# Cross-partition sums and maxima moved from GpSimd to TensorE, and snapshots issued ahead of weight steps

## The chip, the cores and the metric

The kernel runs on one core of a Trainium2 chip. The metric is the device time of one execution in microseconds. The median of three runs of the kernel before is 1585.49 us (1582.71 to 1587.73).

## The reference, cut to what matters

Attention (2 x 8 heads, 768 positions, 64 dimensions, masked to equal clusters) gives x of 1536 x 512. Two networks follow:

```
h = x @ w_in;  x = (h * clip(h + 3, 0, 6) / 6) @ w_out          # first network, w_in 512 x 2048
P = exp(x @ w_gate - max)                                       # 1536 x 8
for _ in range(8):                                              # balancing
    P /= P.sum(1) + 1e-9;  P /= P.sum(0) + 1e-9;  P *= N / E
out = sum over 8 experts e of P[:, e] * (relu(x @ w1[e]) @ w2[e])   # w1: 512 x 1024, w2: 1024 x 512
```

Matrices are multiplied as f16 pairs: a high half and the rest (lo), scaled by a power of two that is taken from the largest absolute value of the whole tensor. So each tensor needs a maximum over all 128 partitions, and each round of balancing a sum over all partitions for 8 columns.

## The kernel before, in words

All engines run their own queues in the order in which the program issues (a manual schedule); an instruction that waits holds all behind it on its engine.

**First network.** w_in and w_out are handled in two halves (n = 0, 1) of 1024 hidden columns. Half 0 runs 24 steps of its first layer (`l1_mm`, then `act2` of the step before and `act1`; L1277 to 1285) and then 24 steps of its second layer (`layer2`, L1307 to 1315). Half 1 does both in one loop with a lag of two steps (L1463 to 1484). Beside them a list `todo` prepares the next weights: load, decode, maximum (`amax`), scale, high and low halves. `run_todo` (L1001) issues in each step a share of the list by listed costs. `hops` (L1013) issues the first part of a maximum in one step, pauses a step or two, and issues all other parts together in one later step (`run`).

A maximum over partitions has two forms. `top_library` (L115): one `partition_all_reduce` on GpSimd (L122), then the scale on VectorE. `top_steps` (L93): VectorE writes each partition's maximum to a column of `pad`; TensorE transposes `pad` into PSUM (`red_rows`, L76); VectorE takes the maximum of each row (`red_max`, L81); TensorE broadcasts the one wanted to all partitions (`to_all`, L86); VectorE computes the scale. Attention uses `top_steps` for the first w_in; all later maxima use `top_library`.

**Experts.** A step n (L1693 to 1721) issues: evacuations of the last step (`evac`), 12 matmuls of the first layer (`l1_part`, L1606 to 1609), 12 of the second layer of a unit 14 steps back (`l2_part`, L1558 to 1560, from step 14 on), the parts of the activation that fall due (`early`), the list `run_todo` (n < 14) and the planned functions `plan2` of the step (weights of coming experts, x2, balancing), and last `post`: snapshots of PSUM sums to SBUF on ScalarE (L1667) and sums on VectorE (L1670 to 1679). An expert takes 42 steps. `l1_part` two steps on writes into a sum again that `post` has copied. Weights: `pre` scales on ScalarE (L1352, L1417), differences and low halves run on GpSimd (L1364 to 1383, L1430, L1438), high halves on ScalarE (L1379, L1434).

**x2 and balancing.** Three blocks of x are scaled anew for the second network (`x2_tasks`): two inside half 1, the third in steps 5 to 25 of the expert loop. `balance_tasks` runs at steps 27 to 51: a maximum over the logits, then eight rounds of `row` (VectorE), `total` (`partition_all_reduce`, L1179, on GpSimd) and `col` (VectorE, which begins with the sum).

Of the kernel before, what the change touches and what calls it, by code (L numbers as in the profile page):

```python
# [31 lines left out]
def attention_moe_kernel(  # L32
# [53 lines left out]
        nc.tensor.matmul(  # L86
            ps, lhsT=r.to_broadcast([P, P]), rhs=ident[:, col:col + ps.shape[1]], start=start, stop=True, skip_group_check=True)

    def sum_all(x, ps):

        nc.tensor.matmul(ps, lhsT=one.to_broadcast([P, P]), rhs=x, start=False, stop=True, skip_group_check=True)

    def top_steps(cols, col, name, room, then):  # L93

# [76 lines left out]
    def spare(n):  # L171
        return spare_columns(n)
# [46 lines left out]
    def weight_tasks(n, m, pool, raw=None):  # L219

        src = layers[n][m]
        wide = src.dtype != F32
        rows, cols = src.shape
        nr = rows // P
        NP = 8
        d = {}
        nm = f"w{n}_{m}"

        def view(t, i):

            return t.rearrange("p a f -> p (a f)")[:, 512 * i:512 * (i + 1)]

        def start():
            d["raw"] = raw
            if raw is None:
                d["raw"] = mp.tile([P, nr, cols], F32, tag="raw", name=f"{nm}_raw", bufs=1)
            d["mx"] = small.tile([P, NP], F32, tag="w_mx", name=f"{nm}_mx")
            if not wide:
                nc.sync.dma_start(d["raw"], src.rearrange("(c p) f -> p c f", p=P))

        def load(i):
            r, o = divmod(512 * i, cols)
            d["c", i] = wide_tile(
                wdec2, src[P * r:P * r + P, o:o + 512].bitcast(U32), f"{nm}_c{i}", [512], bufs=WB)

        def dec0(i):
            d["t", i] = decode0(wdec2, d["c", i], f"{nm}_t{i}", bufs=3)

        def dec1(i):
            decode1(d["t", i])  # L250

        def dec2(i):
            decode2(d.pop(("c", i)), d["t", i], view(d["raw"], i))


        sums = wide and m == 1

        def amax(i):
            if sums:
                nc.scalar.activation(  # L260
                    d.pop(("t", i)).bitcast(F32), view(d["raw"], i), AF.Abs, accum_out=d["mx"][:, i:i + 1])
                return
            nc.vector.tensor_reduce(
                d["mx"][:, i:i + 1], view(d["raw"], i), axis=AX.X, op=ALU.max, apply_absolute_value=True)

        def scale1(m1):
            d["s"], wsc[n, m] = scale_of(m1, 1, 12 if sums else 2 + m, f"ws{m}", small, bufs=4)
            if pool is wpool:
                wsp[n, m] = pool.tile([P, 2, nr, cols], F16, tag="ws", name=f"{nm}_s", bufs=1)
            else:  # L270
                wsp[n, m] = wring[:, 4 * n:4 * n + 4].rearrange("p b x -> p (b x)").rearrange(
                    "p (z r c) -> p z r c", z=2, r=nr)

        def hi(i):
            nc.scalar.activation(view(wsp[n, m][:, 0], i), view(d["raw"], i), AF.Copy, scale=d["s"][:, 0:1])

        def lo(i):
            nc.vector.scalar_tensor_tensor(
                out=view(wsp[n, m][:, 1], i), in0=view(d["raw"], i), scalar=d["s"][:, 0:1],
                in1=view(wsp[n, m][:, 0], i), op0=ALU.mult, op1=ALU.subtract)  # L280

        def piece(i):
            if not wide:
                return idle, idle, idle, idle, lambda: amax(i), idle
            return (lambda: load(i), lambda: dec0(i), lambda: dec1(i), lambda: dec2(i), lambda: amax(i), idle)

        def lo_pool(i):

            v = view(d["raw"], i)
            nc.scalar.activation(v, v, AF.Copy, scale=d["s"][:, 0:1])  # L290
            nc.gpsimd.tensor_tensor(out=view(wsp[n, m][:, 1], i), in0=v, in1=view(wsp[n, m][:, 0], i), op=ALU.subtract)

        parts = []
        for i in range(NP):
            parts += [(0.05, lambda i=i: hi(i)), (0.2, lambda i=i: lo_pool(i)) if (n, m) == (1, 0) else (0.7, lambda i=i: lo(i))]
        scale = top_library(lambda: d["mx"], nm, scale1)
        return start, [("m", piece(i)) for i in range(NP)], scale, parts

    def pipeline(pieces, depth):
# [713 lines left out]
    def hops(steps, turns=1):  # L1013

        def pause():
            pass

        def run():
            for f in steps[1:]:
                f()  # L1020

        far.append(pause)
        return [(0.2, steps[0])] + [(0.0, pause)] * turns + [(1.3, run)]
# [8 lines left out]
    def gate_weights():  # L1032
# [14 lines left out]
            nc.vector.scalar_tensor_tensor(  # L1047
                out=wg[:, 1], in0=raw, scalar=wgs["s"], in1=wg[:, 0], op0=ALU.mult, op1=ALU.subtract)

        return [(0.05, g0), (0.3, g1)] + hops(top_library(lambda: mx, "wg", g1s)) + [(0.3, g2)]  # L1050

    cfac = {}

# [25 lines left out]
    def x2_tasks(bk, room):  # L1079
# [57 lines left out]

        q11, q12, q21, q22 = (0, 0), (0, 1), (1, 0), (1, 1)
        first = [(0.65, lambda h=h, g=g: amax(h, g)) for h in range(2) for g in range(2)]
        top = top_library(lambda: d["mx"], f"x2_{bk}", sc1)  # L1140
        hl = lambda o, v: ([(0.1, hi(o, v))], [(0.7, lo(o, v))])
        order = [
            hl(B11, q11), hl(B21, q21), hl(B22, q22), hl(T1, q11), hl(T3, q12), hl(T2, q22), hl(T4, q21)]
# [12 lines left out]
    def balance_tasks():  # L1156
# [18 lines left out]
            d["cs"] = cs  # L1175

        def total():
            d["ct"] = small.tile([P, NE], F32, tag="b_sum", name="b_sum")
            nc.gpsimd.partition_all_reduce(d["ct"], d.pop("cs"), channels=P, reduce_op=RED.add)  # L1179

        def col(more):
            ct = small.tile([P, NE], F32, tag="b_ct", name="b_ct")
            nc.vector.tensor_scalar(out=ct, in0=d.pop("ct"), scalar1=1e-9, scalar2=None, op0=ALU.add)
            nc.vector.reciprocal(ct, ct)
            nc.vector.tensor_scalar(out=ct, in0=ct, scalar1=float(NT * P) / NE, scalar2=None, op0=ALU.mult)
            nc.vector.tensor_tensor(pr, pr, ct.unsqueeze(1).to_broadcast([P, NT, NE]), op=ALU.mult)
            (row if more else fin)()

# [142 lines left out]
    def expert_w1(e):  # L1331
# [22 lines left out]
        def pair(i):  # L1354
# [33 lines left out]

        return (
            load, [(0.65, lambda i=i: amax(i)) for i in range(8)],  # L1390
            top_library(lambda: d["mx"], f"w{n}_0", scale1), [(0.3, lambda i=i: pre(i)) for i in range(8)],
            [pair(i) for i in range(4)])

    def expert_w2(e):
# [41 lines left out]
        def lo(k, h):  # L1436
# [3 lines left out]

        return (
            load, [(0.3, lambda i=i: amax(i)) for i in range(8)],
            top_library(lambda: d["mx"], f"w{n}_1", scale1), [(0.3, lambda i=i: pre(i)) for i in range(8)],
            diff, hi, lo)

    def parts2(diff, hi, lo):
# [91 lines left out]

    hq, po2, evacs2 = {}, {}, []

    def spare_columns(n):
        return bank(5, "lg2", (n,)), True

    def l2_part(n):

# [135 lines left out]

    first, top, rest = x2_tasks(NBK - 1, spare)
    for n, (_, f) in enumerate(first):
        at2(5 + n, f)
    at2(9, top[0])
    at2(10, top[1])
    for n, (_, f) in enumerate(rest):
        at2(11 + n // 2 if n < len(rest) - 1 else 25, f)
    for n, f in enumerate(balance_tasks()):
        at2(27 + 4 * n // 3, f)  # L1690
    todo += ops2[20:]
    NU2 = 2 * NPASS
    for n in range(PASS * (NPASS + 1)):  # L1693
# [19 lines left out]
                early(u - 1, k + 7)  # L1713
        if u < NU2 and k in (2, 5, 6):
            early(u, k)
        if n < PASS and todo:
            run_todo(max(1, PASS - 3 - n))
        for f in plan2.pop(n, []):
            f()
        if u < NU2:  # L1720
            post(u, k)
    while evacs2:
        evac(*evacs2.pop(0))
    assert not plan2
# [31 lines left out]
```

## Time and profile before

| | |
|---|---|
| median of three runs | 1585.49 us |
| the profiled execution's own time | 1587.1 us |
| its span | 1585.3 us |
| TensorE matmuls, busy share of the span | 88% |
| VectorE, ScalarE, GpSimd | 66%, 57%, 45% |
| mean granted TensorE clock | 0.951 |

The engines are PE (TensorE), DVE (VectorE), ACT (ScalarE), POOL (GpSimd). In the page's 40 slices of 39.6 us TensorE is busy nine tenths or more from slice 21 to slice 39; ahead of that slices 15, 18, 19 and 20 show 5 to 6 tenths, and in the same four the granted clock falls to 7 tenths (counted from 1, read from the left).

### The profile page before, as it was taken

The numbers are of one execution on the slowest core, as the hardware profiler recorded it, in microseconds if no ns is written. First come the engines' busy times: TensorE is split into PE (matmuls) and PEld (weight loads), VectorE is DVE, ScalarE is ACT, GpSimd is POOL, SyncE is SP. The second block draws the span as 40 slices with busy tenths as digits, with TensorE's granted clock in tenths as the row PEclk, the third lists the DMA queues.
The fourth block names the chain that finished last, engine by engine and source line by source line (L and its number), as shares of the span: only waits on it lengthen the run. The fifth ranks groups of instructions, "written<-read, shape, count | busy, mean of one in ns | idle before, by whom it ended". The sixth has DMA issues, their size and how long they took to land.

```text
span 1585.3 us, 30485 instructions
## 1 busy us (share of the span) xinstructions
PE 1390.5 (88%) x12342; PEld 1070.8 (68%) x12342; DVE 1048.0 (66%) x1968; ACT 911.1 (57%) x1633; POOL 714.7 (45%) x721
## 2 busy tenths in 40 slices
PE   3788787898989857965699999999999999999997
PEld 1456565443434326853587888888888888888886
DVE  7788888767755525752467667667676676676664
ACT  3677777464644455442466755756756746756641
POOL 1679889542201555033163363355346426416600
PEclk9999889998999978977799999999999999999999
DMA  9576543322310011000110110110110111011001
GB/s 223 128 157 128 107 87 65 102 94 68 106 53 1 1 53 54 2 1 1 53 39 16 54 47 8 54 54 2 54 54 5 51 54 54 2 55 54 8 28 47
DMA packets 112236, 88.08 MB, mean 56 GB/s; under 512 B 79328, under 2 KB 95712, under 8 KB 112096
## 3 DMA queue, kind: packets, MB, share of 16 engines
q1 hardware_dynamic: 112096, 86.15, 20.1%
q8 instruction: 96, 1.57, 0.4%
q14 instruction: 44, 0.36, 0.1%
HBM read 64.01 MB, written 3.15 MB: 42 GB/s over the span
## 4 chain that ended last, share of the span: by engine, by line
PE 49%; DVE 21%; ACT 12%; issue 9%; POOL 6%; DMA 1%; SPq 0%; DVEq 0%; POOLq 0%; ACTq 0%
PE oX L1558 4%; PE oX L1560 4%; PE oX L1559 4%; PE X L1606 4%; PE X L1608 4%; PE X L1609 4%; DVE pmt L681 3%; PE oY L1558 3%; PE oY L1560 3%; PE oY L1559 3%; ACT w_raw L1352 2%; PE l L1248 2%; ACT w_raw L1417 2%; PE Z L1606 2%; PE Z L1609 2%
## 5 line engine op out<-in xcount | busy, mean ns | idle before, releaser
L748 POOL TENSOR_TENSOR El<-E,Eh 128x384 f16<-128x384 f32 x192 | 189.5, 1017 | 74.4 <-DVE Eh L744 40.6
L1438 POOL TENSOR_TENSOR wring<-w_raw,wring 128x512 f16<-128x512 f32 x112 | 129.3, 1159 | 141.8 <-ACT wring L1434 134.3
L1606 PE MATMUL X<-xop,wop 128*128 128x256 f16 x576 | 160.3, 278 | 30.8 <-ACT snap L1667 24.7
L1608 PEld LDWEIGHTS <-wop 128*128 128x128 f16 x1344 | 133.3, 99 | 71.8 <-issue 54.7
L1577 DVE SCALAR_TENSOR_TENSOR acc<-oX,coef,acc 128x256 f32<-128x256 f32 x168 | 81.0, 482 | 128.5 <-PE oX L1560 118.4
L1608 PE MATMUL X<-xop,wop 128*128 128x256 f16 x576 | 160.4, 278 | 0.0
L1609 PE MATMUL X<-xop,wop 128*128 128x256 f16 x576 | 160.1, 278 | 0.0
L1609 PEld LDWEIGHTS <-wop 128*128 128x128 f16 x1344 | 133.4, 99 | 17.9 <-POOL wop L1383 0.5
L1606 PEld LDWEIGHTS <-wop 128*128 128x128 f16 x1344 | 133.5, 99 | 17.6
L122 POOL PARTITION_ALL_REDUCE w_m<-w_mx x19 | 7.5, 393 | 271.4 <-DVE w_mx L1343 156.4
L735 ACT ACTIVATE E<-pS,esc 128x768 f32<-128x768 f32 x96 | 86.2, 899 | 68.1 <-PE pS L731 46.7
L1606 PE MATMUL Z<-xT,wop 128*128 128x256 f16 x384 | 105.9, 276 | 20.0 <-ACT snap L1667 18.0
L1558 PE MATMUL oX<-wring,a 128*128 128x256 f16 x384 | 105.9, 276 | 16.8 <-ACT acc L1571 12.7
L1615 ACT ACTIVATE a<-a 128x512 f16<-128x512 f32 x96 | 57.4, 598 | 109.7 <-DVE a L1645 71.2
L1615 ACT ACTIVATE q<-u 128x512 f16<-128x512 f32 x96 | 57.1, 595 | 101.9 <-DVE u L1673 77.4
L1558 PE MATMUL oY<-wring,a 128*128 128x256 f16 x384 | 106.0, 276 | 8.2 <-ACT acc L1571 2.9
L1577 DVE SCALAR_TENSOR_TENSOR acc<-oY,coef,acc 128x256 f32<-128x256 f32 x126 | 60.7, 482 | 72.6 <-PE oY L1560 65.4
L1558 PE MATMUL oX<-wring,q 128*128 128x256 f16 x384 | 105.8, 276 | 2.3 <-DVE acc L1577 2.3
L1560 PE MATMUL oY<-wring,a 128*128 128x256 f16 x384 | 106.2, 276 | 0.0
L1559 PE MATMUL oY<-wring,a 128*128 128x256 f16 x384 | 106.1, 276 | 0.0
L1609 PE MATMUL Z<-xT,wop 128*128 128x256 f16 x384 | 106.1, 276 | 0.0
L1608 PE MATMUL Z<-xT,wop 128*128 128x256 f16 x384 | 106.0, 276 | 0.0
(300 smaller groups left out, 4527.5 us busy)
## 6 DMA issues: line engine op xcount, KB each, us to landing
w_raw<-in_moe_w_dram SPq DMA_DIRECT2D x64, 512.0 KB, 5.4
w_c<-in_moe_w_out_dram SPq DMA_DIRECT2D x16, 512.0 KB, 3.3
w00x<-in_moe_w_in_dram SPq DMA_DIRECT2D x8, 512.0 KB, 5.4
w00f<-in_moe_w_in_dram SPq DMA_DIRECT2D x8, 512.0 KB, 4.5
w_c<-in_moe_w_in_dram SPq DMA_DIRECT2D x8, 512.0 KB, 3.9
qraw<-in_q_dram SPq DMA_DIRECT2D x8, 384.0 KB, 3.7
kraw<-in_k_dram SPq DMA_DIRECT2D x8, 384.0 KB, 4.6
vraw<-in_v_dram SPq DMA_DIRECT2D x2, 1536.0 KB, 9.8
```

What stands on the lines that cost most here:

```text
L681: nc.vector.tensor_reduce(nmx[i][:, j:j + 1], ps[:, :, 0:N2], axis=AX.XY, op=ALU.max, negate=True)
L735: nc.scalar.activation(E, ps[:, :, 0:N2], AF.Exp, scale=d["esc"][:, 0:1])
L748: nc.gpsimd.tensor_tensor(out=El[:, g], in0=E[:, g], in1=Eh[:, g], op=ALU.subtract)
L1438: nc.gpsimd.tensor_tensor(out=wop2[k][:, 1, q], in0=value(k)[:, q], in1=wop2[k][:, 0, q], op=ALU.subtract)
L1558: nc.tensor.matmul(o, lhsT=a, rhs=wh, start=(start and t == 0 and i == 0), stop=False, skip_group_check=True)
L1559: nc.tensor.matmul(o, lhsT=a, rhs=wl, start=False, stop=False, skip_group_check=True)
L1560: nc.tensor.matmul(o, lhsT=r, rhs=wh, start=False, stop=(i == 3), skip_group_check=True)
L1577: nc.vector.scalar_tensor_tensor(out=o, in0=v, scalar=coef[e][:, k:k + 1], in1=o, op0=ALU.mult, op1=ALU.add)
L1606: nc.tensor.matmul(r, lhsT=wh, rhs=xh, start=(first and i == 0 and c == 0), stop=False, skip_group_check=True)
L1608: nc.tensor.matmul(r, lhsT=wh, rhs=xl, start=False, stop=False, skip_group_check=True)
L1609: nc.tensor.matmul(r, lhsT=wl, rhs=xh, start=False, stop=(c == 1), skip_group_check=True)
L1615: nc.scalar.activation(h[:, 0], x, AF.Relu if name[0] == "q" else AF.Copy)
```

## The change

The maxima of the first network's weights (but for the first w_in, which had it), of the gate's weights, of the three blocks of x2 and of expert 0's two weights use `top_steps`. The maximum over the logits and those of experts 1 to 7 stay with `partition_all_reduce`. Balancing's sums become a matmul of f32 with ones (`sum_all`). Results go to banks of PSUM that a list `places` names per use. In the expert loop the third block of x2 moves to steps 0 to 20, balancing's maximum to steps 19 to 22 and its rounds to steps 25 to 49, and `post` is issued ahead of `run_todo` and `plan2`.

```diff
-    def sum_all(x, ps):
+    def sum_all(x, ps, start):
-        nc.tensor.matmul(ps, lhsT=one.to_broadcast([P, P]), rhs=x, start=False, stop=True, skip_group_check=True)
+        nc.tensor.matmul(ps, lhsT=one.to_broadcast([P, P]), rhs=x, start=start, stop=True, skip_group_check=True)
...
-        scale = top_library(lambda: d["mx"], nm, scale1)
+        scale = top_steps(lambda: d["mx"], 1, nm, room1, scale1)
...
-        return [(0.05, g0), (0.3, g1)] + hops(top_library(lambda: mx, "wg", g1s)) + [(0.3, g2)]
+        return [(0.05, g0), (0.3, g1)] + hops(top_steps(lambda: mx, 0, "wg", room1, g1s)) + [(0.3, g2)]
...
-        top = top_library(lambda: d["mx"], f"x2_{bk}", sc1)
+        top = top_steps(lambda: d["mx"], 0, f"x2_{bk}", room, sc1)
...
         def total():
-            d["ct"] = small.tile([P, NE], F32, tag="b_sum", name="b_sum")
-            nc.gpsimd.partition_all_reduce(d["ct"], d.pop("cs"), channels=P, reduce_op=RED.add)
+            d["ct"], start = spare(NE)
+            sum_all(d.pop("cs"), d["ct"], start)
...
-            nc.vector.tensor_scalar(out=ct, in0=d.pop("ct"), scalar1=1e-9, scalar2=None, op0=ALU.add)
+            share = NE / float(NT * P)
+            nc.vector.tensor_scalar(
+                out=ct, in0=d.pop("ct"), scalar1=share, scalar2=1e-9 * share, op0=ALU.mult, op1=ALU.add)
             nc.vector.reciprocal(ct, ct)
-            nc.vector.tensor_scalar(out=ct, in0=ct, scalar1=float(NT * P) / NE, scalar2=None, op0=ALU.mult)
...
-            top_library(lambda: d["mx"], f"w{n}_0", scale1), [(0.3, lambda i=i: pre(i)) for i in range(8)],
+            top_library(lambda: d["mx"], f"w{n}_0", scale1) if e else top_steps(
+                lambda: d["mx"], 1, f"w{n}_0", room1, scale1), [(0.3, lambda i=i: pre(i)) for i in range(8)],
...
-            top_library(lambda: d["mx"], f"w{n}_1", scale1), [(0.3, lambda i=i: pre(i)) for i in range(8)],
+            top_library(lambda: d["mx"], f"w{n}_1", scale1) if e else top_steps(
+                lambda: d["mx"], 1, f"w{n}_1", room1, scale1), [(0.3, lambda i=i: pre(i)) for i in range(8)],
...
+    places = []
     def spare_columns(n):
-        return bank(5, "lg2", (n,)), True
+        return bank(places.pop(0), f"free{len(places)}", (n,)), True
...
-        at2(5 + n, f)
-    at2(9, top[0])
-    at2(10, top[1])
-    for n, (_, f) in enumerate(rest):
-        at2(11 + n // 2 if n < len(rest) - 1 else 25, f)
-    for n, f in enumerate(balance_tasks()):
-        at2(27 + 4 * n // 3, f)
+        at2(n, f)
+    for n, f in zip((3, 6, 6, 8, 8), top):
+        at2(n, f)
+    rest = [f for _, f in rest]
+    for n, f in zip((9, 9, 10, 10, 11, 11, 12, 12, 13) + (14, 15, 15, 16, 17, 17, 18, 18, 19, 20), rest[:-1]):
+        at2(n, f)
+    at2(18, rest[-1])
+    more = balance_tasks()
+    for n, f in zip((19, 20, 22), more):
+        at2(n, f)
+    for r in range(8):
+        n = 25 + 7 * (r // 2) + 2 * (r % 2)
+        at2(n, more[3 + 2 * r])
+        at2(n + 1, more[4 + 2 * r])
+    places += [0, 6, 5] + [5, 4] * 4
...
+        if u < NU2:
+            post(u, k)
         if n < PASS and todo:
             run_todo(max(1, PASS - 3 - n))
         for f in plan2.pop(n, []):
             f()
-        if u < NU2:
-            post(u, k)
```

## Rows read from the trace of the kernel before

**Rows 1.** The page, part 1: busy us, share, instructions of each engine.
```profile
PE 1390.5 (88%) x12342; PEld 1070.8 (68%) x12342; DVE 1048.0 (66%) x1968; ACT 911.1 (57%) x1633; POOL 714.7 (45%) x721
```

**Rows 2.** Busy time by stretch: stretch, length, engines' busy us (count), clock, DMA.
```profile
363.90:395.30 31.40, 31.35 (x132) 13.57 (x133) 25.84 (x45) 15.59 (x25) 7.17 (x6) 0.91 0.27 83
582.30:622.60 40.30, 23.15 (x169) 18.21 (x168) 16.99 (x33) 22.58 (x43) 24.73 (x22) 0.83 0.00 1
622.60:696.60 74.00, 70.36 (x642) 61.27 (x640) 50.42 (x105) 40.53 (x81) 13.33 (x16) 0.96 0.08 30
696.60:793.90 97.30, 53.91 (x362) 41.24 (x361) 34.53 (x96) 31.44 (x68) 24.82 (x29) 0.74 0.06 22
1079.55:1192.69 113.14, 110.52 (x1011) 98.61 (x1009) 77.19 (x146) 70.85 (x136) 53.20 (x52) 1.00 0.11 38
```

**Rows 3.** Waits of PE, 696.6 to 793.9: total us, times, longest.
```profile
PE oX L1558 <- ACT acc L1571: 12.3, 2, 8.4
PE X L1606 <- ACT snap L1667: 9.3, 1, 9.3
PE oY L1558 <- ACT acc L1571: 9.1, 1, 9.1
```

**Rows 4.** Waits of POOL, 696.6 to 793.9.
```profile
POOL wop L1383 <- issue: 28.2, 4, 7.2
POOL b_sum L1179 <- issue: 26.0, 4, 8.3
```

**Rows 5.** Order of time, POOL: start, us, instruction, idle before it.
```profile
695.89 0.43 POOL L1179 PARTITION_ALL_REDUCE b_sum<-b_cs  x1 [5.94 <-issue]
703.25 2.11 POOL L1383 TENSOR_TENSOR wop<-cmb,wop 128x1024 f16<-128x1024 f32 x1 [6.94 <-issue]
```

**Rows 6.** Waits of PE, 1079.55 to 1192.69.
```profile
PE Z L1606 <- ACT snap L1667: 1.6, 1, 1.6
PE X L1606 <- ACT snap L1667: 0.9, 1, 0.9
```

**Rows 7.** Lines 76, 81 and 86 (top_steps for w_in): ns min/median/max, starts.
```profile
L76 PE MATMUL w_r<-ident,pad x1: 455/455/455, 141.2 to 141.2; 128*128 128x128 f32 x1
...
L81 DVE TENSOR_REDUCE w_r<-w_r x1: 281/281/281, 143.2 to 143.2; 128x1 f32<-128x128 f32 x1
...
L86 PE MATMUL w_r<-ident,w_r x2: 352/352/353, 171.5 to 171.7; 128*128 128x1 f32 x2
```

**Rows 8.** Order of time, POOL, 610 to 626.
```profile
616.64 0.39 POOL L122 PARTITION_ALL_REDUCE x_m<-x_mx  x1 [5.96 <-issue]
624.51 1.35 POOL L1438 TENSOR_TENSOR wring<-w_raw,wring 128x512 f16<-128x512 f32 x1 [7.48 <-ACT a L1615]
```

**Rows 9.** Order of time, PE, 592 to 681: three gaps.
```profile
592.98 0.37 PE L1606 MATMUL X<-xop,wop 128*128 128x256 f16 x1 [7.86 <-ACT snap L1667]
...
620.15 0.37 PE L1606 MATMUL X<-xop,wop 128*128 128x256 f16 x1 [4.97 <-DVE u L1673]
...
679.98 0.27 PE L1558 MATMUL oY<-wring,a 128*128 128x256 f16 x1 [2.87 <-ACT acc L1571]
```

**Rows 10.** Order of time, ACT, 1091 to 1093.
```profile
1091.42 1.04 ACT L1379 CAST wop<-cmb 128x1024 f16<-128x1024 f32 x1 [1.73 <-POOL cmb L1370]
1092.37 0.58 ACT L1667 COPY snap<-X 128x512 f32<-128x512 f32 x1
```

**Rows 11.** Order of time, PE, first network: three gaps.
```profile
363.95 0.61 PE L1248 MATMUL l<-hh,wring 128*128 128x512 f16 x1 [6.83 <-ACT wring L275]
...
544.64 0.19 PE L1125 MATMUL red<-wg,xT 128*128 128x16 f16 x1 [4.39 <-ACT xT L1107]
...
577.86 0.49 PE L1248 MATMUL l<-hh,w_s 128*128 128x512 f16 x1 [3.77 <-ACT hh L1227]
```

**Rows 12.** Order of time, ACT and DVE: last maxima of two weights.
```profile
345.51 0.19 ACT L260 ACTIVATION_READ_ACCUMULATOR w_t<-w_raw 128x1 f32 x1
...
401.14 0.69 DVE L263 TENSOR_REDUCE w_mx<-w_raw 128x1 f32<-128x512 f32 x1
```

## The prediction

> **What bounds the kernel now.** I read the page's busy shares first, then busy time by stage, then the waits of TensorE and GpSimd, then the order of time. The page has TensorE busy 88% of the span [rows 1], so it is TensorE's gaps that count, and they are not spread evenly. The windows show it [rows 2]. From 1079.55 to 1192.69 one expert (42 steps, 84 half steps of 12 matmuls) takes 113.14 us, of which 2.6 are waits [rows 6]: (113.14 - 2.6)/84 = 1.316 us a half step, 2.63 us a full one. Against this pitch:
> - steps 0 to 13 of the expert loop (half steps, x169 matmuls): 40.3 us for 14 x 1.316 = 18.4, so 21.9 lost;
> - steps 14 to 38 (x642: 600, 40 of the gate, 2 at the edges): 74.0 for 25 x 2.632 = 65.8, 8.2 lost;
> - steps 39 to 53 (x362): 97.3 for 39.5, 57.8 lost, with the granted clock at 0.74.
>
> In the last stretch TensorE waits for ScalarE [rows 3]: for accumulator copies and for a snapshot, three kinds for 30.7 us. These need nothing long of their own; they stand in ScalarE's queue behind halves of weights that wait for GpSimd. GpSimd in turn does little: 24.8 us busy of 97.3, and 28.2 + 26.0 = 54.2 us of its idle time is "issue" before two kinds of instruction [rows 4]. The order of time says which [rows 5]: each reduction of balancing runs 0.43 us, but 5.94 us of nothing stand ahead of it and 6.94 ahead of the next elementwise instruction. So a 0.4 us reduction takes 13.3 us of GpSimd when elementwise work lies on both sides. The Trainium skill ("GPSIMD Engine Reference", section 2.1) says that a freshly loaded library costs some 6 us of invisible load; the 5.94 us agree.
>
> **The change part by part.**
>
> *Balancing's eight sums (L1177).* They leave GpSimd. 97.3 - 54.2 = 43.1 us is what the stretch would take without the "issue" time, close to the 39.5 of the pitch, so GpSimd's chain explains the loss. I keep 5 us for what remains late (accumulator evacuations, VectorE's part of balancing): **-53**. On TensorE each sum is a weight load and matmul of f32 in two passes. No row has 8 columns; the nearest is the broadcast of one column, two passes of 352 ns [rows 7]. Bounds: 0, if it falls into a wait; 0.91 us, two passes as long as the 128-column transpose's 455 ns. I take the nearest, 0.70: 8 x 0.70 = **+5.6**. The sum stands at a step's end on TensorE and its input was made a step before, its reader a step later, so neither queue should stand; behind it in TensorE's queue is the next half step, which both other engines feed on. VectorE loses one small instruction a round. Cost of a missing cover: a lag of a half step in each of eight rounds, 8 x 1.3 = 10 us.
>
> *The third x2 scale and steps 0 to 13.* Before, the maximum ran at 616.64, after 5.96 us idle, and the next GpSimd work began 7.48 us later [rows 8]; VectorE stood for it and TensorE lost 4.97 us [rows 9], at a granted clock of 0.83 over the stretch [rows 2]. That goes: a step or more now lies between the parts of the new form. The other wait of this stretch, 7.86 us at 592.98, is for a snapshot behind a half that waits for GpSimd's differences [rows 9]; the snapshot now goes first. What stays: GpSimd's 22 halves and differences, 24.7 us busy of the 40.3 [rows 2], and ScalarE still stands for them one place further on, so step n's snapshot comes after step n-1's halves. Of 21.9 us lost I take 10 back: **-10** (bounds -18, all but the pipeline's fill, and 0, if the chain of halves sets the end anyhow). What is late next is the same GpSimd chain.
>
> *Steps 14 to 38.* A 2.87 us wait for ScalarE's copy [rows 9], between the first sums, goes with its half clock; the x2 and gate work is moved up to steps 0 to 20, where matmuls are half as dense. 8.2 lost, 3 stay: **-5**. The maximum over the logits stays on GpSimd, at step 20, read at step 22; its load of some 6 us starts when the last difference is done, in step 18 or 19, so a wait of 0 to 3 us on VectorE: 0 taken.
>
> *Snapshots ahead of weights.* In the steady experts TensorE waits 0.9 + 1.6 us for snapshots [rows 6]; the order on ScalarE shows why: a half that waits 1.73 us for GpSimd, and behind it the snapshot [rows 10]. With `post` first the snapshot waits only for its own matmuls. The pattern stands in six experts, in the first of them a little shorter: 6 x 2.5 less 0.5, **-14.5**. The weights' halves move behind, by the rest of the half step at most; they have one to two steps before TensorE reads them, and GpSimd waits for ScalarE there, not the reverse, so 0 (bounds 0 and +14.5, the wait handed to the weights).
>
> *First network's maxima (L296, L1050, L1140, L1391, L1445).* Here the change adds waits: b, c, e and the scale run in one step, so TensorE's two instructions stand at the head of its queue until VectorE has answered, and every later matmul stands behind them.
> - First w_out: TensorE's matmuls end at 363.95 - 6.83 = 357.1; six steps of 31.4 x 0.91/11 = 2.6 us [rows 2] earlier, at 341.5, it would reach the transpose, while ScalarE's last maximum is done at 345.7 [rows 11, 12]. With both engines' next units ahead of the second answer I estimate that it stands until 351: 9.5 us, and 2.8 at half clock (31.4 - 11 x 2.6, what the wait before cost so). In return the 6.83 us wait and its 2.8 of half clock go. **+2.7**.
> - Second w_in, gate and second w_out: TensorE is done with step 10 at 395.3 [rows 2], VectorE has the maxima at 401.8 [rows 12]: 6.5 us of lead. It shrinks to about 0.5, since TensorE comes 2.7 us later and VectorE some 3 earlier (its decoding waited for units that GpSimd's load held). Stalls of 3.3, 1.5 and 1.3 us, 1.5 of half clock, less a wait for w_out's halves behind it that hides most of them: **+1.8** (if the lead stays: +11).
> - First x2 scale and expert 0's w1: a round trip each of 455 + 281 + 704 ns [rows 7] and 0.5 of VectorE's queue, 1.9: **+3.8**.
> - Second x2 scale and expert 0's w2: new stalls of about 4.7 + 2.8 and 2 us; the waits of 4.39 (gate) and 3.77 (hidden layer) [rows 11] go with their half clocks, because GpSimd's load lay ahead of both (4.4 + 2.8 + 3.8 + 2 less 9.5 is 3.5; 2.8 taken): **-2.8**.
>
> Sum -53 + 5.6 - 10 - 5 - 14.5 + 2.7 + 1.8 + 3.8 - 2.8 = -71.4. The profiled execution took 1587.1 us (span 1585.3 and 1.8 around it), within 0.1% of the median 1585.49: 1587.1 - 71.4 = **1515.7**.
>
> **The rivals.**
> 1. *Half of the balance stall stays*: ScalarE's own late work holds TensorE, not GpSimd's loads. For: the waits name ScalarE [rows 3]. Against: 54.2 us of "issue" [rows 4]. 1515.7 + 53/2 = **1542**.
> 2. *The snapshots' gain is handed to the weights*: TensorE waits for wop or wring. For: halves come later. Against: their lead. 1515.7 + 14.5 = **1530**.
> 3. *Slower: TensorE stands in its own queue.* If all 17 reductions (nine maxima, eight sums) cost what the first w_out's does, 9.5 + 2.8 = 12.3 us, that is 209 us against gross gains of 53 + 10 + 5 + 14.5, 9.6 (first w_out) and 12.3 (second x2, hidden layer), 104: 1587 - 104 + 209 = **1692**; it decides from 6.1 us a reduction on. For: one place's lead of 4 us before the answer. Against: in the expert loop a step separates the parts. In the first network's eight alone it gives 98 and 1581.
> 4. *No change*: the loads only fill idle time of GpSimd, and the reductions merely move to the fuller engine. 1587.1 - 14.5 + 5.6 + 5.5 = **1584**. Against: TensorE's waits end when the elementwise instruction behind a load is done. The Trainium skill ("GPSIMD Engine Reference", section 4.1) assigns partition reductions to GPSIMD and would choose the form before; the 0.43 us instruction bears that out, the 13.3 us around it do not.
>
> **How the numbers follow.** Forecast 0.70 (1495 to 1535), half stays 0.11 (1542), handed on 0.11 (1530), slower 0.04, no change 0.04. Between a change and none this measurement can tell about 0.3%, some 5 us: faster 0.92, same 0.04, slower 0.04. Range 1492 to 1545: down to the forecast with 24 us more (8 at the start, 8 in the first network, 5 in balancing, 3 in steps 14 to 38); up to rival 1.
>
> **What would show it.** Right: 15 partition reductions on GpSimd instead of 32; steps 39 to 53 in about 45 us at a clock near 1; no snapshot waits from 860 on, an expert in some 110.7 us; the half steps 0 to 13 in about 30. In the first network, a new gap of TensorE near 342 to 351 and none at 357. Wrong: "issue" time ahead of GpSimd's elementwise work between steps 39 and 53, TensorE waiting for sums, or for wop or wring in the steady experts.

## The result, and the profile after

The changed kernel takes **1504.74 us** (median of 4 runs, 1503.55 to 1505.98) against 1584.1 (4 runs beside it): ratio 0.9496, 95% interval 0.9476 to 0.9515. The forecast was 1515.7, with a range of 1492 to 1545 and a chance of 0.92 for faster. The profiled execution has 1505.1 us, a span of 1503.28; before, the span was 1585.30. The difference of the spans, -82.0, divides over the stretches of the prediction like this. A stretch begins at the first matmul of its step. "First network" is counted from the first layer's first matmul on, because that start itself lies between 288.9 and 293.9 us in the profiles of this study (all the kernels do the same up to there). The stretches are not equally steady: five profiled kernels with the same code there (the changed one and runs 1, 2, 3 and 5) take 288.0 to 289.9 us for the first network, and four (without run 3) 33.4 to 36.4 us for half steps 0 to 13. From step 14 on, kernels with equal code agree within 0.1 us in each stretch.

| stretch | before | after | measured | predicted |
|---|---|---|---|---|
| first network | 289.95 | 289.94 | 0.0 | +5.5 |
| half steps 0 to 13 | 40.32 | 33.36 | -7.0 | -10 |
| steps 14 to 38 | 73.96 | 72.14 | -1.8 | -5, and four sums, +2.8 |
| steps 39 to 53 | 97.33 | 40.32 | -57.0 | -53, and four sums, +2.8 |
| step 54 to the end | 791.34 | 775.16 | -16.2 | -14.5 |

The page's part 1 answers to [rows 1]. TensorE is busy for 17.5 us less: matmuls at half clock have gone.

```profile
PE 1373.0 (91%) x12385; PEld 1066.2 (71%) x12385; DVE 1049.9 (70%) x1970; ACT 914.0 (61%) x1633; POOL 706.2 (47%) x704
```

Busy time by stretch, columns and order as in [rows 2] (the first line is steps 0 to 10 of the second layer, from 368.89; the last one expert). The fourth line is the main result: 15 steps in 40.32 us, 2.69 each, TensorE busy for 40.16 us of that, at a granted clock of 1.00 where it was 0.74. The second is the one that fell short: half steps 0 to 13 still take 33.36 us.

```profile
368.89:398.77 29.88, 29.20 (x136) 13.20 (x135) 25.69 (x47) 10.07 (x16) 2.22 (x2) 1.00 0.43 132
582.30:615.66 33.36, 22.38 (x172) 17.97 (x171) 17.61 (x34) 21.10 (x41) 27.99 (x24) 0.90 0.14 52
615.66:687.80 72.14, 67.87 (x650) 60.28 (x648) 54.00 (x120) 40.84 (x84) 14.31 (x17) 1.00 0.02 7
687.80:728.12 40.32, 40.16 (x371) 35.80 (x368) 30.33 (x73) 29.53 (x65) 16.67 (x17) 1.00 0.17 53
1034.06:1144.45 110.39, 110.19 (x1010) 98.63 (x1008) 77.33 (x145) 71.39 (x136) 53.18 (x53) 1.00 0.12 39
```

TensorE's waits over steps 39 to 53, where [rows 3] had 30.7 us in three kinds:

```profile
PE oX L1563 <- ACT acc L1576: 0.2, 1, 0.2
```

GpSimd's waits there, where [rows 4] had 54.2 us of "issue": now it waits for ScalarE's sums of the next weight, as it should, and nothing is put down to "issue".

```profile
POOL w_m L122 <- ACT wring L1411: 11.4, 1, 11.4
POOL wop L1384 <- ACT wop L1380: 3.1, 5, 2.1
```

Partition reductions are left on GpSimd as forecast, 15 of 32: these 14 (the page's part 5: count, busy us, mean ns, idle before) and the one over the logits.

```profile
L122 POOL PARTITION_ALL_REDUCE w_m<-w_mx x14 | 5.6, 398 | 223.2 <-DVE w_mx L1344 142.2
```

TensorE's waits in the steady expert 1034.06 to 1144.45, for [rows 6]: the snapshots are gone, and no wait for wop or wring came in their place.

```profile
PE oX L1563 <- DVE acc L1582: 0.2, 1, 0.2
```

The first network, order of time on TensorE, for the first of [rows 11]: the new gaps stand where the prediction put them (341.5 to 351; they end at 350.00), and after the first layer there is no gap any more.

```profile
346.03 0.38 PE L76 MATMUL red<-ident,pad 128*128 128x128 f32 x1 [4.46 <-DVE pad L100]
350.00 0.59 PE L86 MATMUL red<-ident,w_r 128*128 128x1 f32 x2 [3.60 <-DVE w_r L81]
```

Order of time on TensorE, half steps 2 to 12, for the first of [rows 9]: the wait for a snapshot, 7.86 us before, is still 3.85, and TensorE waits for three more snapshots behind it. ScalarE's order of time, below, shows the cause of the first: it waits 3.79 us for GpSimd's differences ahead of that snapshot (and 2.11 ahead of the third).

```profile
592.85 0.37 PE L1611 MATMUL X<-xop,wop 128*128 128x256 f16 x1 [3.85 <-ACT snap L1672]
...
604.44 0.27 PE L1611 MATMUL X<-xop,wop 128*128 128x256 f16 x1 [1.59 <-ACT snap L1672]
...
610.37 0.27 PE L1611 MATMUL X<-xop,wop 128*128 128x256 f16 x1 [2.42 <-ACT snap L1672]
613.05 0.27 PE L1611 MATMUL Z<-xT,wop 128*128 128x256 f16 x1 [1.21 <-ACT snap L1672]
```
```profile
589.96 0.62 ACT L1436 CAST wring<-w_raw 128x512 f16<-128x512 f32 x1 [3.79 <-POOL w_raw L1432]
...
592.24 0.56 ACT L1672 COPY snap<-X 128x512 f32<-128x512 f32 x1
```

Line 91, the sums: duration in ns (min/median/max) and starts of the 16 passes of eight sums, and in the order of time the first sum with the matmuls on either side. The next half step starts 0.14 us after the sum does, though the row has 0.29 for both passes: records of neighbouring matmuls overlap, so the price of a sum is read from start to start and not from its duration.

```profile
L91 PE MATMUL free<-b_cs,one x16: 175/252/256, 648.7 to 714.6; 128*128 128x8 f32 x16
```
```profile
648.60 0.27 PE L1565 MATMUL oY<-wring,a 128*128 128x256 f16 x1
648.71 0.29 PE L91 MATMUL free<-b_cs,one 128*128 128x8 f32 x2
648.85 0.27 PE L1611 MATMUL Z<-xT,wop 128*128 128x256 f16 x1
```

### The profile page after: what moved, and what is told of

It reads as the page before. It is cut to its first block, busy times and chain, and to the rows that moved or that the text cites. A ratio compares the mean times of both kernels' runs of the same rounds, so it can differ in the third digit from the quotient of the medians.

```text
span 1503.3 us, 30515 instructions
## 1 busy us (share of the span) xinstructions
PE 1373.0 (91%) x12385; PEld 1066.2 (71%) x12385; DVE 1049.9 (70%) x1970; ACT 914.0 (61%) x1633; POOL 706.2 (47%) x704
## 4 chain that ended last, share of the span: by engine, by line
PE 62%; DVE 20%; ACT 6%; issue 4%; POOL 3%; DMA 1%; SPq 0%; DVEq 0%; POOLq 0%; ACTq 0%
PE oX L1563 5%; PE oX L1565 5%; PE oX L1564 5%; PE X L1614 5%; PE X L1611 5%; PE X L1613 5%; PE oY L1563 4%; PE oY L1564 4%; PE oY L1565 4%; DVE pmt L681 3%; PE l L1249 3%; PE Z L1611 2%; PE Z L1613 2%; PE Z L1614 2%; DVE w_mx L1344 2%
## 5 line engine op out<-in xcount | busy, mean ns | idle before, releaser
L1611 PE MATMUL X<-xop,wop 128*128 128x256 f16 x576 | 157.6, 274 | 9.0 <-ACT snap L1672 9.0
L1613 PE MATMUL X<-xop,wop 128*128 128x256 f16 x576 | 157.7, 274 | 0.0
L1614 PE MATMUL X<-xop,wop 128*128 128x256 f16 x576 | 157.6, 274 | 0.0
L1563 PE MATMUL oX<-wring,a 128*128 128x256 f16 x384 | 104.6, 272 | 6.1 <-DVE acc L1582 4.2
L1563 PE MATMUL oY<-wring,a 128*128 128x256 f16 x384 | 104.6, 273 | 4.5 <-DVE acc L1582 3.4
L1565 PE MATMUL oY<-wring,a 128*128 128x256 f16 x384 | 104.7, 273 | 0.0
L1565 PE MATMUL oX<-wring,a 128*128 128x256 f16 x384 | 104.7, 273 | 0.0
L1564 PE MATMUL oY<-wring,a 128*128 128x256 f16 x384 | 104.7, 273 | 0.0
```

The lines of the kernel that those rows point to most:

```text
L1563: nc.tensor.matmul(o, lhsT=a, rhs=wh, start=(start and t == 0 and i == 0), stop=False, skip_group_check=True)
L1564: nc.tensor.matmul(o, lhsT=a, rhs=wl, start=False, stop=False, skip_group_check=True)
L1565: nc.tensor.matmul(o, lhsT=r, rhs=wh, start=False, stop=(i == 3), skip_group_check=True)
L1611: nc.tensor.matmul(r, lhsT=wh, rhs=xh, start=(first and i == 0 and c == 0), stop=False, skip_group_check=True)
L1613: nc.tensor.matmul(r, lhsT=wh, rhs=xl, start=False, stop=False, skip_group_check=True)
L1614: nc.tensor.matmul(r, lhsT=wl, rhs=xh, start=False, stop=(c == 1), skip_group_check=True)
```

## The experiments

The theory: a partition reduction between elementwise work takes 13 us from GpSimd, ScalarE's queue stands behind that, and TensorE behind ScalarE. The first rival: the order of the queues (snapshots, places of the rounds) was what hurt. After the result two more questions were open: why the first network cost nothing, and why half steps 0 to 13 gained no more. Comparisons by stretch are with the table above. In brackets behind a run's time stand its ratio to the kernel before, measured beside it, and the 95% interval of that ratio.

**1. The sums back on GpSimd** (all else as changed):
```
-            d["ct"], start = spare(NE)
-            sum_all(d.pop("cs"), d["ct"], start)
+            d["ct"] = small.tile([P, NE], F32, tag="b_sum", name="b_sum")
+            nc.gpsimd.partition_all_reduce(d["ct"], d.pop("cs"), channels=P, reduce_op=RED.add)
```


> The changed kernel, with the eight sums of balancing made again by a partition reduction on GpSimd, at the changed kernel's own steps (20, 25 to 48); all else as changed. Theory (each reduction stops GpSimd's chain of weights for about 13.3 us, 5.94 before and 6.94 after it): steps 39 to 53, 40.3 us in the changed kernel, get back some of the 57 us that they lost, less because the rounds now start at step 25 and are spread over 26 steps: steps 14 to 53 together +40 to +57, total 1545 to 1562, with 'issue' time ahead of GpSimd's elementwise work. Rival (the stall went because snapshots come first and the rounds are spread): +10 at most, total below 1515.

**2. The sums on TensorE, and the reductions as well, unread:**
```
+            unread = small.tile([P, NE], F32, tag="b_sum", name="b_sum")
+            nc.gpsimd.partition_all_reduce(unread, d["cs"], channels=P, reduce_op=RED.add)
             d["ct"], start = spare(NE)
```


> The changed kernel, with the sums on TensorE as they are, and beside each of the eight a partition reduction on GpSimd of the same input into a tile that nobody reads. Theory (what hurts is what the reduction does to GpSimd's other work, not when the sum's answer comes): the time of the run with the sums back on GpSimd, within 6 us. Rival (balancing's own chain, VectorE waiting for the answer and the matmul queue behind it): the time of the changed kernel, 1505, plus at most 5.

Run 1: **1541.5** (0.9718, 0.9685 to 0.9751), 36.8 over the changed kernel. Run 2: **1532.8** (0.9664, 0.9634 to 0.9694), 28.1 over it. By stretch, steps 14 to 38 have +5.9 and +6.3, steps 39 to 53 +30.4 and +23.1, the other stretches nothing beyond what equal code differs by. So eight reductions that nobody waits for cost 29 of the 36 us: it is what they do to GpSimd's other work. Run 1 lies a little under its bound of 40, run 2 9 below run 1 in the medians and 7 in the stretches, where at most 6 were expected. Those 7 are the answer's own path, at one place in run 1: VectorE waits for the seventh sum, ScalarE 5.33 us for VectorE's a, TensorE 5.09 for ScalarE's copy. VectorE's waits, 737 to 765, in run 1; run 2 has no such wait:
```profile
DVE b_ct L1184 <- POOL b_sum L1179: 7.3, 1, 7.3
```
GpSimd's order of time in run 1 tells why the 36 us are not 8 x 13.3 = 106:
```profile
650.28 0.40 POOL L1179 PARTITION_ALL_REDUCE b_sum<-b_cs  x1 [10.71 <-DVE b_cs L1174]
...
670.44 0.40 POOL L1179 PARTITION_ALL_REDUCE b_sum<-b_cs  x1 [7.86 <-DVE b_cs L1174]
677.47 0.71 POOL L1365 TENSOR_TENSOR cmb<-w_raw 128x256 f32<-128x256 f32 x1 [6.64 <-issue]
...
697.24 0.43 POOL L1179 PARTITION_ALL_REDUCE b_sum<-b_cs  x1 [5.74 <-issue]
704.73 2.11 POOL L1384 TENSOR_TENSOR wop<-wring,wop 128x1024 f16<-128x1024 f32 x1 [7.06 <-issue]
...
715.68 0.43 POOL L1179 PARTITION_ALL_REDUCE b_sum<-b_cs  x1 [5.99 <-issue]
723.09 1.78 POOL L1384 TENSOR_TENSOR wop<-w_raw,wop 128x512 f16<-128x512 f32 x2 [6.97 <-ACT wop L1380]
```
From 639 to 670 the first four rounds find GpSimd without elementwise work: TensorE loses nothing up to step 36. The next elementwise instruction then starts 6.64 us after the fourth reduction is done. The fifth and sixth round, amid elementwise work, cost 5.74 and 5.99 us ahead of them and 7.06 and 6.97 behind; the last two come close together, with 9.05 us ahead of the first. From 682 to 765, as in the kernel before, TensorE waits for ScalarE's copies (9.5 and 9.3 us) and a snapshot (6.3).

**3. Snapshots after the weights' steps again; 4. the kernel before with the snapshots first** (the same two lines moved, back in the changed kernel, ahead in the one before; shown is run 4):
```
+        if u < NU2:
+            post(u, k)
         if n < PASS and todo:
             run_todo(max(1, PASS - 3 - n))
         for f in plan2.pop(n, []):
             f()
-        if u < NU2:
-            post(u, k)
```


> The changed kernel, with a half step's snapshots issued after the weights' steps again, as before. Theory (snapshots stood behind halves that wait for GpSimd): the steady experts take 113.1 us instead of 110.4 and steps 0 to 13 some 5 us more, total +16 to +23, 1521 to 1528; no stall like the one of balancing (at most 5 us more in steps 39 to 53). Rival (order alone carried much of balancing's stall): over 20 us more in steps 39 to 53, total above 1535.

> The kernel before, with the half step's snapshots ahead of the weights' steps and nothing else changed. Theory: the steady experts gain 16, steps 0 to 13 about 5; the stall of balancing shrinks by at most 10 of its 57, since accumulator copies still stand behind halves that wait for GpSimd: total 1584 less 18 to 30, 1554 to 1566. Rival (the snapshots' place was what made the reductions hurt): balancing's stretch loses 30 or more of its stall, total below 1545.

Run 3: **1523.2** (0.9602, 0.9575 to 0.9630), 18.5 over the changed kernel. Run 4: **1566.1** (0.9871, 0.9842 to 0.9900), 19.9 under the one before. The totals fit the theory: run 3 lies in its range, run 4 at the upper end. In run 3 steps 39 to 53 take 41.5 us: with no reductions, the stall does not need the snapshots' order to be gone. In run 4 they take 89.7, 7.6 of 57 less, and GpSimd's "issue" time is that of [rows 4] again:
```profile
POOL wop L1383 <- issue: 28.3, 4, 7.4
POOL b_sum L1179 <- issue: 25.9, 4, 8.5
```
From step 54 on run 3 loses 16.5 us, run 4 gains 14.8. Half steps 0 to 13 are the surprise: run 4 takes 40.53 us there, 0.2 more than before, run 3 34.67. Equal code differs by up to 3 us in this stretch, so neither run shows a gain from the snapshots' place that is clear of this. What took it from some 40 us to 33 to 36 came with the third x2 block: its maximum in the new form and its earlier steps. No run separates those two.

**5. The price of a sum** (each of the eight done nine times):
```
+            cs = d.pop("cs")
+            for _ in range(9):
+                sum_all(cs, d["ct"], start)
```


> The changed kernel, with each of balancing's eight sums made nine times over into the same place, 64 more of them (the last stays, so the values are the same). It prices a sum on TensorE. By the prediction's 0.70 us a sum: 64 x 0.70 = +45, total 1550. By the 0.14 us by which a step with a sum is longer than one without (2.76 for 2.62) in the profile of the changed kernel: 64 x 0.14 = +9, total 1514. Above 45: the repeated sums also wait for something, and a gap of TensorE names it.

**1515.6** (0.9550, 0.9517 to 0.9583), 10.8 over the changed kernel. From step 25 to step 54 the profile has 9.7 us more for 64 sums: 0.15 us each on balance, not 0.70. That is an average of two things. Steps 39 to 53, where TensorE had nothing to wait for, are 7.0 us longer for 32 sums, 0.22 each; steps 25 to 38 only 2.7, because TensorE's waits of 1.42, 1.10, 0.51 and 0.80 us there are gone. The starts say the same: nine sums in a row take 1.93 us from the first pass to the next matmul.
```profile
717.76 2.07 PE L91 MATMUL free<-b_cs,one 128*128 128x8 f32 x18
719.69 0.27 PE L1613 MATMUL Z<-xT,wop 128*128 128x256 f16 x1
```
A single sum in the changed kernel takes 0.14 us by starts in seven of the eight places and 0.21 in the other: 1.2 us for all eight.

**6. The first network's eight maxima back on GpSimd** (one of five such edits; the third x2 keeps the new form):
```
-        scale = top_steps(lambda: d["mx"], 1, nm, room1, scale1)
+        scale = top_library(lambda: d["mx"], nm, scale1)
```


> The changed kernel, with the eight maxima of the first network's stretch (its weights, the gate, the first two x2 scales, both weights of expert 0) made on GpSimd again; the third x2 scale, the sums and the snapshots stay as changed. By the prediction's sum these eight cost 5.5 net, so this would be 5.5 faster, 1499. Theory after the trace (the chain on ScalarE and VectorE sets this stretch in either form, TensorE's wait only moves): the expert loop starts within 2 us of the changed kernel's 582.3, total 1505 plus or minus 3. Rival (what TensorE loses early it got back because GpSimd's loads no longer hold VectorE later): the loop starts some 5 us later or more, total 1510.

**1503.7** (0.9480, 0.9451 to 0.9508), the changed kernel's time. First network: 289.10 us here; over all the profiles the old form has 288.8 to 290.0 (three kernels, mean 289.3), the new one 288.0 to 290.1 (nine, without run 7, mean 289.1). Whatever the form costs is lost in the 1.9 us by which equal code differs. Neither the forecast's 5.5 nor the rival's 5 is there.

**7. The first w_out's parts in steps of their own:**
```
-    todo += pipeline(pcs, {"m": WB}) + hops(scale, 2) + parts[:12]
+    todo += pipeline(pcs, {"m": WB}) + hops(scale, 4, 2) + parts[:12]
...
+        def ask():
+            for f in steps[1:3]:
+                f()
+        def answer():
+            for f in steps[3:]:
+                f()
+        if mid:
+            return [(0.2, steps[0])] + [(0.0, pause)] * turns + [(0.7, ask)] + [(0.0, pause)] * mid + [(0.6, answer)]
```


> The changed kernel, with the parts of the first w_out's maximum in steps of their own: TensorE's first instruction four turns after the maxima in place of two, its second two turns after the first. Theory (a second chain sets the stretch): TensorE's gaps of 4.46 and 3.60 us at 341.6 and 346.4 and the half clock behind them go, some 10 us at that place, but second layer and second half wait for ScalarE and VectorE: from 8 to 10 us at the first layer's end shrink to under 3 by the start of the expert loop, total 1502 to 1506. Rival (the in-order wait really costs what it takes): 8 or more are kept to the end, total 1497 or less.

**1504.9** (0.9485, 0.9456 to 0.9514): no gain. The second layer starts 7.6 us earlier than in the changed kernel (361.27 for 368.89, with the same start of the first layer); at 446.05, in the second half, 1.6 of it is left, and the expert loop starts 1.6 later. TensorE's order of time shows where most of it went back: at the next weight's maximum, for which the changed kernel waits 0.30 us and this one 3.49:
```profile
393.41 0.45 PE L76 MATMUL red<-ident,pad 128*128 128x128 f32 x1 [3.49 <-DVE pad L100]
```

**8. Low halves of expert 0's second weight on VectorE; 9. four of its eight sums on VectorE:**
```
-            nc.gpsimd.tensor_tensor(
+            (nc.gpsimd if e else nc.vector).tensor_tensor(
                 out=wop2[k][:, 1, q], in0=value(k)[:, q], in1=wop2[k][:, 0, q], op=ALU.subtract)
```
```
+            if e == 0 and i % 2:
+                nc.vector.tensor_reduce(
+                    d["mx"][:, i:i + 1], d["raw"][:, i], axis=AX.X, op=ALU.add, apply_absolute_value=True)
+                return
             nc.scalar.activation(
```


> The changed kernel, with the low halves of expert 0's second weight on VectorE in place of GpSimd, fourteen of them: 0.69 us each there for 1.13. Theory (GpSimd's unbroken chain of halves and differences, 584.2 to 609.9, sets steps 0 to 13): the chain shrinks to its eight differences, some 10 us of work, and steps 0 to 13, 33.4 us in the changed kernel for 18.4 at the steady pitch, take 25 to 28: total 1497 to 1500. Rival (VectorE's and ScalarE's own work there, or the pipeline's fill, sets them): within 2 us of 33.4, total 1505; slower, if VectorE now stands for ScalarE's halves: up to 1510.

> The changed kernel, with four of the eight column sums of expert 0's second weight made on VectorE (0.67 us each there) in place of ScalarE (8 us for all eight, 568.3 to 576.3). Theory (the last gap ahead of the expert loop, 5.45 us at 571.1 for pad, is paid in full: the chain from the load over the sums, the scale and the prepared weight to GpSimd's first half at 584.2 sets the start): the gap shrinks to 1 to 2, GpSimd starts some 4 us sooner, and the loop with it: total 1499 to 1502. Rival (VectorE takes its four late, since it stands there for ScalarE's u, or the loop waits for the second layer's last evacuations anyhow): within 1 us, total 1504 to 1506.

Run 8: **1499.7** (0.9457, 0.9427 to 0.9487; the interval overlaps the changed kernel's). Half steps 0 to 13 take 31.09 us for 33.36: 2.3 less, close to the rival's 2 and far from the theory's 25 to 28 us. The rest of the 6.8 us by which its profile is shorter was there before the expert loop (3.5 is an earlier start of the first layer). The stretch in the columns of [rows 2]:
```profile
577.63:608.72 31.09, 20.12 (x173) 16.69 (x172) 28.56 (x47) 21.41 (x40) 14.15 (x10) 1.00 0.09 30
```
GpSimd's 27.99 us are halved, but VectorE is now busy for 28.56 of 31.09 us, so it leaves no room for more. The run says that this way out is closed, not what held the stretch before. Run 9: **1503.5** (0.9478, 0.9454 to 0.9501), nothing, the rival's case: the sums follow the transfers, which land 1.3 us apart, and VectorE's last one stands behind u, 0.68 us at 575.77.

**10. Expert 0's second weight spread over steps 0 to 16; 11. the same, paced by time:**
```
-            todo += ops2[:20]
+            todo.append((4.0, nothing))
...
-    todo += ops2[20:]
+    todo += ops2
...
-        if n < PASS and todo:
-            run_todo(max(1, PASS - 3 - n))
+        if todo:
+            run_todo(max(1, 17 - n))                               # 10
+            run_todo(22 - n if n < 14 else max(1, 18 - n))         # 11
```
(and in the list of pieces each high half is followed by its low half, differences at 1.2, low halves at 1.1, high ones at 0.05 of cost)

> The changed kernel, with the differences and halves of expert 0's second weight spread over steps 0 to 16 of the expert loop (before: twenty of them all at the end of the first network, the rest by step 10), each half of a part with its own low half behind it; the amount of work is the same. Theory (steps 0 to 13 are long because the halves stand in ScalarE's queue all at once and wait there for GpSimd, not because GpSimd's 25 us are too much): snapshots come on time, steps 0 to 13 take 22 to 28 us in place of 33.4, and no wait for the second weight follows at steps 14 to 20: total 1494 to 1500. Rival (GpSimd's chain, or the serial work on ScalarE and VectorE in the first two units, sets the time): within 3 us of 33.4, or the wait comes back at steps 14 to 20 for wring: total 1502 to 1508.

> The version that steps 0 to 13 point to: as the run with the second weight's pieces spread, but paced evenly in time (one piece of GpSimd's a half step up to step 13, two a full step from 14 to 17), since in that run GpSimd still had its pieces without a break from 582 to 598 and ScalarE stood for it up to 2.4 us at a time. Theory (ScalarE's standing in order is what is left): the gap of 3.73 us at 592.6 for a snapshot goes, steps 0 to 15 take 29 to 31 us for 32.5, total 1492 to 1495. Rival (the serial work of the first units on ScalarE and VectorE is what is left, or the halves now come late for steps 14 to 20): no gain, 1495 to 1499.

Run 10: **1495.7** (0.9433, 0.9413 to 0.9453); run 11: **1494.4** (5 runs, 1491.67 to 1497.59; 0.9425, 0.9406 to 0.9445). Both lie below the changed kernel's interval; between the two the medians tell nothing. Half steps 0 to 13, the columns of [rows 2]: first run 10, then run 11.
```profile
578.94:605.63 26.69, 21.50 (x172) 17.95 (x171) 16.99 (x32) 18.75 (x36) 20.66 (x18) 0.86 0.00 1
```
```profile
577.78:598.43 20.65, 18.90 (x172) 16.67 (x171) 17.02 (x33) 17.37 (x33) 14.88 (x13) 1.00 0.01 2
```
Half steps 0 to 13 take 33.36, 26.69 and 20.65 us in the changed kernel and in runs 10 and 11, where 14 half steps at the steady pitch take 18.4. Steps 14 to 38 then take 72.14, 73.21 and 75.82, so part of run 11's gain goes back (waits of 1.3 us for copies at 603.85 and 617.52). Run 11's only gap of TensorE in the first fourteen is
```profile
595.81 0.27 PE L1609 MATMUL Z<-xT,wop 128*128 128x256 f16 x1 [1.55 <-ACT snap L1670]
```
The theory holds, somewhat more strongly than expected (in run 11 steps 0 to 15 take 27.4 us, not 29 to 31). The same work on the same engines, issued one piece at a time in place of twenty at once, gives most of the 15 us that were still lost there. The pieces held the stretch because ScalarE waited for them in order, ahead of the snapshots; the weight itself isn't read before step 14, so that its pieces can come as late as run 11 lets them. Two things changed along with the spreading and were not separated from it: each low half now follows its high half, and some of GpSimd's work now falls after step 13 (it is busy for 27.99, 20.66 and 14.88 us of the stretch).

## Why the prediction was right, point by point

- **Balancing: right, and for the reason given.** -53 forecast, -57.0 measured with four sums in it; the 5 us kept for what remains late did not come, TensorE is busy for 40.16 of 40.32 us. Rival 1 (ScalarE's own late work) falls with run 2: reductions that nobody reads bring 23 us back into steps 39 to 53; rival 4 (loads fill idle time) holds only for the rounds that meet an idle GpSimd, up to 670 in run 1. What the forecast did not separate: the 57 are not the reductions' alone. With the changed kernel's order and places they cost 30.4 in this stretch (run 1; 36 with steps 14 to 38); the remaining 27 go with the earlier, wider places of the rounds and the snapshots first, of which run 4 shows 7.6 for the snapshots. The division of the other 19 was not tried.
- **Sums on TensorE: mis-sized.** +5.6 forecast, +1.2 measured (eight sums by their starts, and about the 0.15 a sum of run 5). The price was read wrongly from the row, two passes of 352 ns [rows 7]: in the kernel before, these stand between attention's matmuls, take 0.43 us from their start to the next matmul's, and run at a granted clock of 0.50, the lower of its two levels (1.2 GHz). So 0.70 counts the overlap twice, and the slow clock besides; the sums of balancing ran at 1.00.
```profile
171.19 0.52 PE L763 MATMUL pv<-vn,El 128*128 128x65 f16 x6
171.52 0.57 PE L86 MATMUL w_r<-ident,w_r 128*128 128x1 f32 x2
171.94 0.80 PE L678 MATMUL pmt<-kA,qA 80*128 80x384 f16 x2
```
```profile
171.00:172.30 1.30, 1.30 (x17) 1.13 (x15) 0.36 (x1) 1.30 (x2) 1.30 (x2) 0.50 1.11 204
```
- **Half steps 0 to 13: direction right, one cause wrong.** -7.0 for -10. The third x2 block gave nearly all of it (runs 3 and 4); the gap of 4.97 us [rows 9] is gone. The snapshots' place was to remove the other wait, of 7.86 us; it gave nothing clear of the 3 us by which equal code differs, because ScalarE still waited for GpSimd one half earlier in its queue. "What is late next is the same GpSimd chain" was half of it: it counts when its pieces stand in ScalarE's queue all at once, and hardly when they are spread (runs 10 and 11).
- **Steps 14 to 38: over-sized.** -1.8 for -5. The 2.87 us wait went, but waits of 1.42 us at 664.98 (for VectorE's sum) and 1.10 at 671.62 (for ScalarE's copy) came. With the snapshots last, run 3 takes 70.32 us here, 1.8 less than the changed kernel: here their new place costs time.
- **Snapshots in the steady experts: right.** -16.2 for -14.5, an expert 110.39 us for the 110.7 forecast. Rival 2 (the gain handed to the weights) is excluded by the waits of this stretch, 0.2 us, none for wop or wring.
- **First network: 0.0 for +5.5, and the term that failed is the second.** First w_out: the second layer's step 10, the last ahead of the next maximum, starts 2.1 us later (2.7 forecast). From there to the second half's third second-layer step, where +1.8 was forecast, it is -2.3. Before, TensorE waited there for halves of a weight, shown by its order of time in the kernel before:
```profile
440.77 0.39 PE L1248 MATMUL l<-hh,w_s 128*128 128x512 f16 x1 [3.85 <-ACT w_s L275]
```
The stretch around it, 428.99 to 447.94, took 18.95 us at a clock of 0.91; after the change it takes 12.95 (434.74 to 447.69) at 1.00, 6.0 less. The forecast had 7.6 us of stalls and half clock, of which this wait would hide 5.8. The 5.8 was right; the 7.6 was not: from start to start the three maxima of second w_in, gate and second w_out cost 1.4, 0.9 and 1.4 us, 3.7 in all and at full clock, with gaps of 0.3 to 0.4. The first x2 scale and expert 0's w1 then cost 2.8 (3.8 forecast), the last two -2.6 (-2.8). That costs and refunds add up to 0.0 so exactly is luck: kernels with equal code differ by 1.9 us here. That a gain at one place is taken back at the next is shown by run 7.
- **Rival 3 (TensorE in its own queue)** is real where TensorE reaches a maximum before VectorE has it ready: 8.06 us of gaps at the first w_out (9.5 forecast), 3.42 at the second x2 scale (4.7 forecast), 5.84 at expert 0's w2 (2 forecast). It did not decide, since the other five maxima of this stretch have gaps of 0.4 to 1.0 us each, and at the last two places the waits of [rows 11] went in return; 3.49 us came back in run 7 as soon as TensorE was early again. The gaps of the last two places:
```profile
533.52 0.33 PE L76 MATMUL red<-ident,pad 128*128 128x128 f32 x1 [1.58 <-DVE pad L100]
535.69 0.38 PE L86 MATMUL red<-ident,x_r 128*128 128x1 f32 x2 [1.84 <-DVE x_r L81]
576.59 0.45 PE L76 MATMUL red<-ident,pad 128*128 128x128 f32 x1 [5.45 <-DVE pad L100]
577.42 0.59 PE L86 MATMUL red<-ident,w_r 128*128 128x1 f32 x2 [0.38 <-DVE w_r L81]
```

The sum was 10.6 us short of the span's change (-71.4 against -82.0): the terms missed by -4.6 (balancing, four sums taken out), -4.4 (sums), +3.0 (half steps 0 to 13), +2.6 (14 to 38, four sums taken out), -1.7 (snapshots) and -5.5 (first network).

## What to carry to other kernels

Price a partition reduction on GpSimd by what stands next to it: among elementwise work it took 13 us of GpSimd here, in a stretch where GpSimd was idle it cost TensorE nothing; and look for the engine whose queue stands behind it, which is the one that the waits name. When an in-order queue waits for another engine, spread the pieces over the steps before moving them to a third engine: the same halves, one at a time, were worth 7 to 13 us in fourteen half steps (5.6 to 9.0 left at step 21); fourteen of them moved to VectorE, 2. Price a short matmul by the time from its start to the next one's, at the clock at which it will run. A gap that is removed early in a chain of stages counts only by how much earlier the last stage starts.

## What the runs showed of the hardware

- An f32 matmul of 8 columns, two passes of 175 to 256 ns in the records, took 0.14 us of TensorE's time amid other matmuls, from start to start at a granted clock of 1.00 (the changed kernel, seven of eight); eight more in a row behind it took 0.22 each (run 5).
- GpSimd's return from a reduction to elementwise work took 6.6 to 7.1 us in run 1 (6.64, 7.06, 6.97). Nothing of it shows where the next input comes later than that: in the changed kernel GpSimd's first elementwise instruction after a reduction starts 0.1 us after the ScalarE instruction it waits for, which ends at 676.84.
```profile
664.70 0.40 POOL L122 PARTITION_ALL_REDUCE w_m<-w_mx  x1 [31.39 <-DVE w_mx L1344]
676.93 0.73 POOL L1365 TENSOR_TENSOR cmb<-w_raw 128x256 f32<-128x256 f32 x1 [11.83 <-ACT w_raw L1353]
```
- The granted clock of a stretch does not follow from its code, nor from its lost time alone. Half steps 0 to 13, in the columns of [rows 2], of runs 1 and 5, which have the same code there, show 0.95 and 0.81. The kernel before, the changed one and runs 8, 10 and 11 lost 21.9, 15.0, 12.7, 8.3 and 2.3 us there, at 0.83, 0.90, 1.00, 0.86 and 1.00.
```profile
579.07:612.92 33.85, 21.46 (x172) 17.50 (x171) 17.61 (x34) 21.58 (x41) 28.00 (x24) 0.95 0.14 51
581.71:618.08 36.37, 25.13 (x172) 19.30 (x171) 18.87 (x35) 22.78 (x43) 28.80 (x25) 0.81 0.16 59
```
